# Decode attention with a Mish layer on one core: keys and values moved as whole 8 MiB units on one queue

## The chip, the cores and the metric

The kernel runs on one NeuronCore of one Trainium2 chip. The metric is the device time of one execution in microseconds (us), lower is better. Device memory feeds the core's on-chip memory (128 partitions) through 16 DMA engines. TensorE (PE) multiplies, VectorE (DVE) and ScalarE (ACT) work on the results, GpSimd (POOL) only clears buffers here, SyncE (SP) issues transfers. TensorE's products land in PSUM, in banks of 128 partitions by 512 f32.

## The reference

One decode step for 8 sequences, all f32. `x` is 8 rows of 512; 32 query heads share 8 key/value heads (4 per group); the caches hold 8192 positions of 128 numbers for each sequence and key/value head, 256 MiB of keys and 256 MiB of values.

```python
xn = layernorm(x)                                   # eps 1e-5
q  = (xn @ wq) as 8 x 32 heads x 128
p  = softmax(q . k * 128**-0.5)                     # over 8192 positions
o  = p . v
h  = xn @ w1 + b1                                   # 512 -> 1792
out = x + o @ wo + mish(h) @ w2                     # mish(h) = h * tanh(softplus(h))
```

The host lays the arrays out beforehand: keys in 1024 blocks of 128 dims x 1024 positions, values in 1024 blocks of 128 x 1024 numbers, 8 blocks for each sequence and head.

## The kernel before

The work is a list of items (L479 to L502), each a transfer into one of nine 16 KiB-per-partition buffers named `kv` (L54, L81) and the work on it. Key units `(n, b, s)` are half the positions of one head and one sequence, 2 MiB; value units are the same halves in another order. The first 16 items of keys (all sequences and halves of head 0) run alone; from then on key units of head n+1 and value units of head n alternate, and at the end 16 value units run alone. The query weights `wq` come in four pieces, two heads each, spread over the run; `wo` comes in eight pieces, one per head; `w1` after the fourth key unit; `w2` in three pieces last. The loop at L505 issues each item's transfer six items ahead (`AHEAD`), alternating between SP's and ACT's queue (`transfer`, L84), then emits the item's work.

In a key unit a row, the piece that one partition holds contiguously, is 8 KiB (L98 to L105), in a value unit 16 KiB (L107 to L114). `project` (L196) forms the queries of one head for all sequences. `scores` (L235) multiplies a key unit with weights of 64 columns; two products share the array. All 8 sequences of a head accumulate side by side in the two-bank tiles `S[0]`, `S[1]`. After the last of them `maximum` (L258) and `weights` (L272) run once per head: the maximum over rows by two tiny transposes on PE, `exp` on ACT, and a 32x32 block transpose on DVE (L284) that brings the exponents `pt` to the partitions on which the values lie. `sums` (L294) adds up the denominators, `values` (L301) multiplies exponents with value units, four products side by side, into `O`, and picks the wanted blocks with four DVE operations (L317, L319). `merge` (L330) and `outputs` (L343) apply `wo` per head; `mish` (L368) and `down` (L419) are the dense layer, `mish` right after `w1` has come, `down` at the end. Engines wait for each other by semaphores that the Tile framework puts in; each engine works through its own instructions in order.

Of the kernel before, what the change touches and what calls it, by code (L numbers as in the profile page):

```python
# [14 lines left out]
B = 8  # L15
# [7 lines left out]

G = 4
NH = 2
UK = SK // NH
GK = UK // G
TG = GK // P
# [8 lines left out]

R = B * REP
PU = NH * B

KA = 2
WK = KA * R
QB = KA * WK
QBUFS = 3
W = BW * G // DH
W4 = 4
W2R = G * FT // 2 * FP // P  # L50

BUFS = 9
AHEAD = 6
# [3 lines left out]
def kernel(  # L57
# [16 lines left out]
    kv = ctx.enter_context(tc.tile_pool(name="kv", bufs=BUFS))  # L74
# [6 lines left out]
    def buffer():  # L81
        return kv.tile([P, G * BW], F32, name="kv")

    def transfer(t, src):  # L84

        queues.reverse()
        queues[0].dma_start(t, src)

    def load_blocks(src, lo, n):

        _, rows, width = src.shape
        t = buffer()[:rows, : n * width].rearrange("p (j f) -> p j f", j=n)
        transfer(t, src[lo : lo + n].rearrange("j p f -> p j f"))
        return t

    def load_k(n, b, s):
        lo = ((b * HKV + n) * NH + s) * G
        t = buffer().rearrange("p (j f) -> p j f", j=G // KA)  # L98
        transfer(
            t,  # L100
            kT[lo : lo + G]
            .rearrange("(j a) p f -> j (a p f)", a=KA)
            .rearrange("j (p f) -> p j f", p=P),
        )
        return t  # L105

    def load_v(n, b, s):  # L107

        lo = ((b * HKV + n) * NH + s) * G
        t = buffer()  # L110
        transfer(
            t, v[lo : lo + G].rearrange("j p f -> (j p f)").rearrange("(p f) -> p f", p=P)
        )
        return t  # L114

    w2_rows = w2.rearrange("j p f -> (j p) f").rearrange("(q i) f -> q (i f)", i=W2R)

    def load_w2(lo, hi):

        t = buffer()[:, : (hi - lo) * BW]  # L120
        transfer(t, w2_rows[:, lo * BW : hi * BW])
        return t

    x_sb = const.tile([B, D], F32, name="x_sb")
    nc.scalar.dma_start(x_sb, x)
    b1_sb = const.tile([G, FG], F32, name="b1_sb")
    nc.scalar.dma_start(b1_sb, b1.rearrange("(g f) -> g f", g=G))


    items = []  # L130


    S = [psum.tile([P, GK], F32, name=f"s{i}") for i in range(NH)]
    O = [psum.tile([P, 512], F32, name=f"o{i}") for i in range(2)]
# [4 lines left out]
    ones = const.tile([P, P], F32, name="ones")  # L139

    gsel = const.tile([G, G, B], F32, name="gsel")

    rsel = const.tile([P, R], F32, name="rsel")

    hsel = const.tile([P, REP], F32, name="hsel")

    isel = const.tile([P, W4], F32, name="isel")
    qT = [const.tile([P, B * (QB + 1)], F32, name=f"qT{i}") for i in range(QBUFS)]
    xnT = const.tile([P, CC, B], F32, name="xnT")
    acc = const.tile([P, P], F32, name="acc")  # L150
    aT = const.tile([P, 2 * W2R, Q], F32, name="aT")

    def setup():
        make_identity(nc, ident)
        nc.gpsimd.memset(ones, 1.0)
        for t in qT:
            nc.gpsimd.memset(t, 0.0)
        nc.vector.memset(M, 0.0)
        nc.vector.memset(H, 0.0)
        for o in O:  # L160
            nc.vector.memset(o, 0.0)

        st = const.tile([B, 8], F32, name="st")
        xc = const.tile([B, D], F32, name="xc")
        sq = const.tile([B, D], F32, name="sq")
        nc.vector.reduce_sum(st[:, 0:1], x_sb, axis=AX.X)
        nc.vector.tensor_scalar_mul(st[:, 1:2], st[:, 0:1], 1.0 / D)
        nc.vector.tensor_scalar(xc, x_sb, st[:, 1:2], None, op0=ALU.subtract)
        nc.scalar.activation(sq, xc, AF.Square, accum_out=st[:, 2:3])
        nc.vector.tensor_scalar(  # L170
            st[:, 3:4], st[:, 2:3], 1.0 / D, EPS, op0=ALU.mult, op1=ALU.add
        )
        nc.scalar.activation(st[:, 4:5], st[:, 3:4], AF.Sqrt)
        nc.vector.reciprocal(st[:, 5:6], st[:, 4:5])

        nc.vector.tensor_mul(st[:, 6:7], st[:, 5:6], st[:, 5:6])
        nc.vector.tensor_mul(st[:, 7:8], st[:, 6:7], st[:, 3:4])
        nc.vector.tensor_scalar(st[:, 6:7], st[:, 7:8], -0.5, 1.5, op0=ALU.mult, op1=ALU.add)
        nc.vector.tensor_mul(st[:, 4:5], st[:, 6:7], st[:, 5:6])
        nc.vector.tensor_scalar(xc, xc, st[:, 4:5], None, op0=ALU.mult)  # L180
        for c in range(CC):
            nc.tensor.transpose(  # L182
                M[:, c * B : (c + 1) * B], xc[:, c * P : (c + 1) * P], ident[:B, :B]
            )
        nc.vector.tensor_copy(xnT.rearrange("p c b -> p (c b)"), M[:, : CC * B])

        nc.vector.tensor_copy(
            gsel, ident[:G, :G].rearrange("p (g o) -> p g o", o=1).to_broadcast([G, G, B])
        )
        nc.vector.reduce_sum(rsel, ident.rearrange("p (g r) -> p r g", g=G), axis=AX.X)  # L190
        used = rsel[:, : W4 * REP]
        nc.vector.reduce_sum(hsel, used.rearrange("p (i h) -> p h i", h=REP), axis=AX.X)
        nc.vector.reduce_sum(isel, used.rearrange("p (i h) -> p i h", h=REP), axis=AX.X)


    def project(n, w):  # L196

        for c in range(CC):
            for h in range(REP):
                lo = (n % 2 * REP + h) * DH  # L200
                nc.tensor.matmul(  # L201
                    H[Q * h : Q * h + B, 384:512],
                    xnT[:, c, :],
                    w[:, c, lo : lo + DH],
                    start=(c == 0),
                    stop=(c == CC - 1),
                )

        qs = work.tile([P, KA, KA, DH // KA], F32, name="qs")
        for a in range(KA):  # L210
            nc.vector.tensor_scalar_mul(  # L211
                qs[:, :, a, :],
                H[:, 384:512].rearrange("p (i r) -> p r i", r=KA),
                DH**-0.5,
            )
        for k in range(KA):
            nc.tensor.transpose(  # L217
                H[:, k * P : (k + 1) * P], qs[:, k].rearrange("p a i -> p (a i)"), ident
            )

        t = qT[n % QBUFS].rearrange("p (b c) -> p c b", c=QB + 1)
        half = P // KA
        for a in range(KA):
            for k in range(KA):
                lo = k * WK + a * R
                nc.vector.tensor_copy(  # L226
                    t[half * a : half * (a + 1), lo : lo + R : B, :],
                    H[half * a : half * (a + 1), k * P : (k + 1) * P].rearrange(
                        "p (h q) -> p h q", h=REP
                    )[:, :, :B],  # L230
                )

    NM = {}

    def scores(n, b, s, k):  # L235

        for c in range(GK // 512):
            for i in range(KA):
                w = QB * b + WK * i
                for j in range(G // KA):  # L240
                    at = i * BW + c * 512
                    nc.tensor.matmul(  # L242
                        S[s][WK * j : WK * (j + 1), c * 512 : (c + 1) * 512],
                        qT[n % QBUFS][:, w : w + WK],
                        k[:, j, at : at + 512],
                        start=(b == 0 and i == 0),
                        stop=(b == B - 1 and i == KA - 1),
                    )
        if b == B - 1:
            if s == 0:  # L250
                NM[n] = work.tile([P, NH], F32, name="nm")
            nc.vector.tensor_reduce(  # L252
                NM[n][:, s : s + 1], S[s], axis=AX.X, op=ALU.max, negate=True
            )

    NX, PT, RT = {}, {}, {}

    def maximum(n):  # L258

        nmb = work.tile([P, 1], F32, name="nmb")  # L260
        nc.vector.tensor_reduce(nmb, NM[n], axis=AX.X, op=ALU.min)
        nc.tensor.transpose(M[:1, 0:P], nmb, ident)
        nr = work.tile([1, Q], F32, name="nr")
        nc.vector.tensor_reduce(
            nr, M[:1, 0:P].rearrange("p (g q) -> p q g", g=G), axis=AX.X, op=ALU.min
        )
        nx = NX[n] = work.tile([1, G, Q], F32, name="nx")
        nc.vector.tensor_copy(
            nx, nr.rearrange("p (o q) -> p o q", o=1).to_broadcast([1, G, Q])
        )  # L270
# [286 lines left out]
```

## Time and profile before

| what | value |
|---|---|
| time, median of 3 runs | 1342.06 us (1341.81 to 1342.19) |
| profiled execution, span from first to last instruction | 1340.1 us |
| moved by DMA | 561.81 MB, mean 419 GB/s over the span |
| busy: PE, PE weight loads, DVE, ACT, POOL | 920.3, 267.1, 179.1, 23.8, 3.5 us |
| mean granted TensorE clock | 0.843 |

The profile is of one execution, whose span is 2 us shorter than the median time. Its page cuts the span in 40 equal slices (33.5 us each); a digit is the busy share in tenths, GB/s is what the DMA engines moved. A line of a group names source line, engine, operation, output <- inputs, shapes and count, then total busy time, mean ns of one, and idle time before it with what ended it. A line of the timeline begins with start and length in us and merges equal instructions (`x16`). A line of windows gives, for a stretch of time, the busy time of each engine, the granted TensorE clock, the DMA share and GB/s. A line of DMA issues ends with KB each and the median us from issue to landing. f32 products show as two instructions each.

### The profile page before, as it was taken

The page shows a single profiled execution, that of the slowest core. Times are in us where ns is not written, and L with a number is a line of the kernel's source. Part 1 is how long each engine was busy: PE and PEld are TensorE (multiplying, and loading weights), DVE is VectorE, ACT ScalarE, POOL GpSimd, SP SyncE. Part 2 cuts the span into 40 slices and gives each one's busy share as a digit, 9 for nine tenths or more (in the row PEclk, how much of TensorE's full clock was granted, in tenths as well). Part 3 has the DMA queues.
Part 4 walks back from the last instruction along what each step waited for, and adds up shares of the span by engine and source line. Part 5 has one row for each costly group of instructions (what it writes and reads, how often), then busy time and mean ns, then how long its engine had stood idle before and what let it go on. Part 6 is the DMA issues. An engine that isn't in the chain of part 4 may idle for free.

```text
span 1340.1 us, 11019 instructions
## 1 busy us (share of the span) xinstructions
PE 920.3 (69%) x4948; PEld 267.1 (20%) x4948; DVE 179.1 (13%) x443; ACT 23.8 (2%) x39; POOL 3.5 (0%) x10
## 2 busy tenths in 40 slices
PE   3778759574766856766667776676757687567766
PEld 1222212121112212212112221221212122112212
DVE  2212011020100201111010120102100020010311
ACT  1000000000000000000000000000000000000000
POOL 1000000000000000000000000000000000000000
PEclk9888879797788967988787897887878888788878
DMA  9999999999999999999999999999999999999996
GB/s 385 419 422 424 426 421 424 422 425 425 426 424 420 427 423 423 424 423 425 425 426 427 419 425 422 423 426 422 424 425 424 424 424 427 424 423 424 428 427 269
DMA packets 59240, 561.81 MB, mean 419 GB/s; under 512 B 4396, under 2 KB 4528, under 8 KB 9784
## 3 DMA queue, kind: packets, MB, share of 16 engines
q10 hardware_dynamic: 29608, 281.31, 50.0%
q1 hardware_dynamic: 29584, 279.78, 49.8%
q8 instruction: 39, 0.64, 0.2%
q14 instruction: 9, 0.07, 0.0%
HBM read 561.01 MB, written 0.07 MB: 419 GB/s over the span
## 4 chain that ended last, share of the span: by engine, by line
DMA 78%; PE 17%; another core or an unknown queue 4%; DVE 1%; issue 0%; ACTq 0%; ACT 0%; SPq 0%
DMA kv<-in_kT 62%; DMA kv<-in_v 12%; PE s L242 10%; PE o L308 5%; DMA kv<-in_w 2%; DMA kv<-in_wq 1%; PE h L201 1%; PE h L423 0%; PE m L356 0%; PE m L332 0%; PE h L217 0%; DVE pt L284 0%; PE m L295 0%; DVE os L317 0%
## 5 line engine op out<-in xcount | busy, mean ns | idle before, releaser
L242 PE MATMUL s<-kv,qT 128*64 128x512 f32 x2048 | 603.2, 730 | 307.3 <-DMA kv<-in_kT 303.7
L242 PEld LDWEIGHTS s<-kv,qT 128*64 128x64 f32 x2048 | 166.4, 166 | 711.4 <-DMA kv<-in_kT 369.6
L308 PE MATMUL o<-kv,pt 128*16 128x512 f32 x2048 | 265.5, 624 | 41.4 <-DMA kv<-in_v 39.1
L317 DVE TENSOR_SCALAR os<-o,isel 128x128 f32<-128x128 f32 x64 | 22.5, 351 | 703.2 <-PE o L308 703.2
L308 PEld LDWEIGHTS o<-kv,pt 128*16 128x16 f32 x2048 | 56.2, 114 | 190.3 <-issue 139.9
L319 DVE SCALAR_TENSOR_TENSOR os<-o,isel,os 128x128 f32<-128x128 f32 x192 | 67.1, 350 | 6.2
L252 DVE TENSOR_REDUCE nm<-s 128x1 f32<-128x1024 f32 x16 | 19.6, 1225 | 298.7 <-PE s L242 298.7
L283 ACT ACTIVATE e<-s,nmx 128x1024 f32<-128x1024 f32 x16 | 17.7, 1110 | 1187.6 <-DVE nmx L277 864.5
L201 PE MATMUL h<-kv,xnT 128*8 128x128 f32 x256 | 12.7, 362 | 37.2 <-DMA kv<-in_wq 37.2
L284 DVE STREAM_TRANSPOSE pt<-e 128x1024 f32<-128x1024 f32 x16 | 31.6, 2018 | 1.4 <-ACT e L283 1.3
L332 PEld LDWEIGHTS m<-hsel,os 128*128 128x128 f32 x128 | 19.3, 190 | 59.8 <-issue 44.9
L332 PE MATMUL m<-hsel,os 128*128 128x4 f32 x128 | 24.9, 265 | 8.5 <-DVE os L319 8.5
L201 PEld LDWEIGHTS h<-kv,xnT 128*8 128x8 f32 x256 | 7.7, 112 | 46.3 <-DMA kv<-in_wq 28.7
L211 DVE TENSOR_SCALAR qs<-h 128x128 f32<-128x128 f32 x16 | 4.2, 286 | 49.9 <-PE h L201 49.9
L356 PE MATMUL m<-kv,oT 128*8 128x128 f32 x256 | 8.9, 275 | 0.3 <-DVE oT L337 0.3
L378 PE MATMUL h<-kv,xnT 128*8 128x448 f32 x32 | 4.9, 742 | 6.0 <-DMA kv<-in_w 6.0
L356 PEld LDWEIGHTS m<-kv,oT 128*8 128x8 f32 x256 | 6.2, 89 | 5.3 <-DVE r L297 4.4
L226 DVE COPY qT<-h 64x32 f32<-64x32 f32 x32 | 5.0, 208 | 15.1 <-PE h L217 15.0
L423 PE MATMUL h<-kv,aT 128*8 128x128 f32 x112 | 5.9, 406 | 1.0 <-DMA kv<-in_w 1.0
L297 DVE RECIPROCAL r<-m 128x32 f32<-128x32 f32 x8 | 2.9, 358 | 27.1 <-PE m L295 27.1
L182 PE MATMUL m<-ident,xc 8*128 8x8 f32 x4 | 0.6, 247 | 8.2 <-DVE xc L180 8.2
L423 PEld LDWEIGHTS h<-kv,aT 128*8 128x8 f32 x112 | 4.1, 132 | 2.9 <-DMA kv<-in_w 1.4
(72 smaller groups left out, 62.1 us busy)
## 6 DMA issues: line engine op xcount, KB each, us to landing
kv<-in_kT SPq DMA_DIRECT2D x64, 2048.0 KB, 34.1
kv<-in_kT ACTq DMA_DIRECT2D x64, 2048.0 KB, 38.5
kv<-in_v ACTq DMA_DIRECT2D x64, 2048.0 KB, 27.9
kv<-in_v SPq DMA_DIRECT2D x64, 2048.0 KB, 27.9
kv<-in_wq ACTq DMA_DIRECT2D x2, 2048.0 KB, 18.2
kv<-in_wq SPq DMA_DIRECT2D x2, 2048.0 KB, 51.1
kv<-in_wo ACTq DMA_DIRECT2D x4, 1024.0 KB, 40.5
kv<-in_wo SPq DMA_DIRECT2D x4, 1024.0 KB, 35.9
```

The lines of the kernel that those rows point to most:

```text
L201: nc.tensor.matmul(H[Q * h : Q * h + B, 384:512], xnT[:, c, :], w[:, c, lo : lo + DH], start=(c == 0), stop=(c == CC - 1),)
L226: nc.vector.tensor_copy(t[half * a : half * (a + 1), lo : lo + R : B, :], H[half * a : half * (a + 1), k * P : (k + 1) * P].rearrange("p ( ...
L242: nc.tensor.matmul(S[s][WK * j : WK * (j + 1), c * 512 : (c + 1) * 512], qT[n % QBUFS][:, w : w + WK], k[:, j, at : at + 512], start=(b == ...
L252: nc.vector.tensor_reduce(NM[n][:, s : s + 1], S[s], axis=AX.X, op=ALU.max, negate=True)
L283: nc.scalar.activation(e[:, s], S[s], AF.Exp, bias=nmx, accum_out=l[:, s : s + 1])
L284: nc.vector.transpose(pt[:, s].rearrange("p (m t r) -> p t m r", m=m, t=TG), e[:, s].rearrange("p (t q m) -> p t m q", t=TG, m=m),)
L308: nc.tensor.matmul(o[Q * c : Q * c + W4 * REP, :], PT[n][:, s, W4 * R * j + b : W4 * R * (j + 1) : B], vt[:, 512 * j : 512 * (j + 1)], sta ...
L317: nc.vector.tensor_scalar(os, o[:, :DH], isel[:, 0:1], None, op0=ALU.mult)
L319: nc.vector.scalar_tensor_tensor(os, o[:, DH * i : DH * (i + 1)], isel[:, i : i + 1], os, op0=ALU.mult, op1=ALU.add,)
L332: nc.tensor.matmul(M[:, 168 + b * REP : 168 + (b + 1) * REP], OS.pop((n, b)), hsel, start=True, stop=True)
L356: nc.tensor.matmul(M[Q * g : Q * g + B, 256:384], oT[n][:, h, :], w[:, h // 2, h % 2 * D + g * P : h % 2 * D + (g + 1) * P], start=(h == 0 ...
L423: nc.tensor.matmul(H[Q * g : Q * g + B, :P], aT[:, j, :B], w[:, at : at + P], start=(j == 0), stop=(j == 2 * W2R - 1),)
```

## The change

The whole schedule is rewritten; the host's layout and the result are the same. A **unit** is now one sequence `b` and a pair of heads `m`: 16 blocks, 8 MiB of keys or of values, moved by one transfer in which each partition gets 64 KiB (`ROW`) contiguously. There are 32 units. All transfers but the two smallest (`x`, `b1`) are issued by SP. On-chip there is one array `kv` of 160 KiB per partition: keys of even units at 0, of odd ones at 32 KiB, so that neighbouring units share half their place, and one place for values behind them. Three of the four `wq` pieces come first, into the place of the values, then the first keys, then `w1` and the last `wq` piece.

```diff
-BUFS = 9
-AHEAD = 6
+NB = 2 * NH * G                  (16 blocks a unit)
+ROW = NB * P * BW // P           (16384 f32)
+DI = ROW // BW                   (16)
+K_AT = (0, ROW // 2)
+V_AT = ROW + ROW // 2
+PLACES = V_AT + ROW
...
-    queues = [nc.sync, nc.scalar]
+    ctx.enter_context(tc.manual_schedule())
+    kv = const.tile([P, PLACES], F32, name="kv")
+    S = psum.tile([P, 512], F32, name="s")
+    X = psum.tile([P, 4, 512], F32, name="x4")
+    O = psum.tile([P, 512], F32, name="o")
...
+    def load_pair(src, m, at):
+        t = kv[:, at : at + 4096]
+        rows = src.rearrange("j p f -> (j p f)").rearrange("(m p f) -> m p f", m=NP, p=P)
+        nc.sync.dma_start(t, rows[m])
+    def load_unit(src, j, at):
+        m, b = divmod(j, B)
+        lo = (b * HKV + 2 * m) * NH * G
+        t = kv[:, at : at + ROW]
+        nc.sync.dma_start(t, src[lo : lo + NB].rearrange("j p f -> (j p f)")
+                             .rearrange("(p f) -> p f", p=P))
...
+    def project(m):
+        for d in range(2):
+            for c in range(CC):
+                nc.tensor.matmul(H[Q * c : Q * c + B, :], xn4[:, c, :],
+                                 w[:, c, d * 512 : (d + 1) * 512], start=True, stop=True)
+            nc.scalar.copy(qp, H)
+            for h in range(REP):
+                nc.tensor.matmul(M[:, at : at + B], qp[:, h * DH : (h + 1) * DH], bsel[:, :B], ...)
+        nc.vector.tensor_scalar_mul(qT, M[:, 192 : 192 + H2 * B], DH**-0.5)
+        for half in range(2):
+            for k in range(8):
+                nc.tensor.matmul(X[:, half, k * 64 : (k + 1) * 64], wide[:, half * 8 + k :: DI], qT, ...)
+            nc.scalar.copy(qr[:, m, half * 8 : (half + 1) * 8]..., X[:, half])
+    def key_weights(j):
+        for d in range(2):
+            nc.vector.tensor_mul(w[:, :, d], q[:, :, d]..., mask[...]...)      (512 elements each)
+    def scores(j, k, first, part):
+        lo = 0 if first else DI // 2
+        for n in range(DI // 2):
+            for c in range(HALF):
+                nc.tensor.matmul(S[64 * c : 64 * (c + 1), :], w[:, lo + n]..., kk[:, lo + n, c, :],
+                                 start=(part == 0 and n == 0), stop=(part == 1 and n == DI // 2 - 1))
+    def softmax(j):        (maximum of S, two transposes on PE, exp of 128 x 512 on ACT, lsel)
+    def turn(j, lsel):
+        for g in range(4):
+            nc.tensor.matmul(X[:, g], perm[:, g], e, start=True, stop=True)
+        nc.tensor.matmul(M[:, 136 : 136 + H2], ones, lsel, start=True, stop=True)
+        nc.vector.reciprocal(RT[j], M[:, 136 : 136 + H2])
+        for tl in range(TL):
+            nc.vector.transpose(tr...[:, tl], X...[:, tl])                   (512 elements each)
+        for d in range(2):
+            nc.vector.tensor_reduce(pt8[half...], tr[half]..., axis=AX.X, op=ALU.add)  (2048 in)
+    def values(j, vt):     (32 products of 32 columns into O, then the four DVE operations)
+    def merge(j, os):
+        nc.tensor.matmul(M[:, 168 : 168 + H2], os, hsel, start=True, stop=True)
+        nc.vector.tensor_mul(oT[:, m, :, b], M[:, 168 : 168 + H2], RT.pop(j))
...
+    for m in range(NP - 1):
+        project(m)
+        if m == 0:
+            key_weights(0)
+    (w1, b1 and the last piece of wq are loaded)
+    for j in range(UNITS):
+        scores(j, k, j % 2 == 1, 0)
+        if j + 1 < UNITS:
+            k_t[j + 1] = load_k(j + 1)
+        else:
+            v_t[j] = load_unit(v, j, 0)
+        scores(j, k, j % 2 == 0, 1)
+        lsel = softmax(j)
+        if j > 0:
+            os = values(j - 1, v_t.pop(j - 1))
+        else:
+            mish(w1_t, b1_sb, kv[:, V_AT + 8192 : V_AT + 12288 - FG])
+            project(NP - 1)
+        if j + 1 < UNITS:
+            v_t[j] = load_unit(v, j, V_AT)
+            key_weights(j + 1)
+        turn(j, lsel)
+        if j > 0:
+            merge(j - 1, os)
+    (wo in four pieces into the place of the values, w2 in three into that of the keys)
+    (values of the last unit, all output products into X[:, 0], down per piece of w2)
```

The text in round brackets stands for code that is left out or for sizes. The scores of a unit fill one bank, `S`: its 128 rows are two halves of 512 positions, two heads, eight blocks and four query heads. Exponents and values of a unit lie on different partitions; `turn` brings them together with four products against the permutation matrices `perm`, four block transposes and two reductions, where before one block transpose per half did it. The setup also builds `perm` (eight small copies), `mask`, `bsel`, `isel`, `rsel` and `hsel` (six reductions), `wide` and a second set of transposed inputs, `xn4`. `mish` is unchanged but keeps its intermediate tiles in the place of the values. The products with `wo` all run after the last unit, and their result is added to `H` by four products with `bsel`.

More of the change, by code (lines that the diff above doesn't have):

```diff
@@ L196, in project @@
[L196 to L270, printed above, removed]
@@ new lines @@
+    for c in range(CC):
+        nc.tensor.transpose(
+            M[:, 32 + c * B : 32 + (c + 1) * B], xc[:, c * P : (c + 1) * P], ident[:B, :B]
+        )
+    nc.vector.tensor_copy(xn4.rearrange("p c b -> p (c b)"), M[:, 0:32])
+    nc.vector.tensor_copy(xnT.rearrange("p c b -> p (c b)"), M[:, 32:64])
+    for g in range(G):
+        nc.tensor.matmul(
+            M[Q * g : Q * g + B, 256:384],
+            ident[:B, :B],
+            x_sb[:, g * P : (g + 1) * P],
+            start=True,
+            stop=True,
+        )
@@ L368, in mish @@
-    def mish(ws):
+                tr.rearrange("p (l t) c -> p t l c", t=TL)[:, tl],
+                X.rearrange("p g (t q l) -> p t l g q", t=TL, q=PP)[:, tl],
+            )
+        for d in range(2):
+            half = slice(64 * d, 64 * (d + 1))
+            nc.vector.tensor_reduce(
+                pt8[half, :, :, d * REP : (d + 1) * REP].rearrange("p c y h -> p y c h"),
+                tr[half].rearrange("p y (g c h) -> p y c h g", g=4, c=HALF),
+                axis=AX.X,
+                op=ALU.add,
+            )
@@ new lines, in values @@
+    def values(j, vt):
+        for n in range(NJ):
+            l, c = divmod(n, HALF)
+            q = n % G
+            nc.tensor.matmul(
+                O[Q * q : Q * (q + 1), :],
+                pt8[:, c, TL * l : TL * (l + 1), :].rearrange("p t h -> p (t h)"),
+                vt[:, 512 * n : 512 * (n + 1)],
+                start=(n < G),
+                stop=(n >= NJ - G),
+            )
+        os = work.tile([P, DH], F32, name="os")
+        nc.vector.tensor_scalar(os, O[:, :DH], isel[:, 0:1], None, op0=ALU.mult)
+        for i in range(1, TL):
+            nc.vector.scalar_tensor_tensor(
+                os, O[:, DH * i : DH * (i + 1)], isel[:, i : i + 1], os, op0=ALU.mult, op1=ALU.add
+            )
+        return os
@@ new lines @@
+    os = values(UNITS - 1, v_t.pop(UNITS - 1))
+    for m in range(NP - 1):
+        outputs(m, w_o[m])
+    merge(UNITS - 1, os)
+    outputs(NP - 1, w_o[NP - 1])
+    a_sb = work.tile([P, 512], F32, name="e")
+    nc.scalar.copy(a_sb, A)
+    down(*parts[0], w2_t[0])
+    for g in range(G):
+        nc.tensor.matmul(
+            H[Q * g : Q * g + B, :P],
+            bsel[:, :B],
+            a_sb[:, g * P : (g + 1) * P],
+            start=False,
+            stop=False,
+        )
+    for p, t in zip(parts[1:], w2_t[1:]):
+        down(*p, t)
@@ L516 @@
     res = const.tile([P, P], F32, name="res")
[L517 removed]
+    nc.vector.tensor_add(res, H[:, :P], xres)
     nc.sync.dma_start(out, res)
```

441 lines of the change are left out of this document (196 added, 245 removed).

## The prediction, made before the changed kernel was run

> **What bounds the kernel now.** First the page: its slices, its queues and the chain that ended last.
>
> ```profile
> PEclk9888879797788967988787897887878888788878
> DMA  9999999999999999999999999999999999999996
> GB/s 385 419 422 424 426 421 424 422 425 425 426 424 420 427 423 423 424 423 425 425 426 427 419 425 422 423 426 422 424 425 424 424 424 427 424 423 424 428 427 269
> ...
> q10 hardware_dynamic: 29608, 281.31, 50.0%
> q1 hardware_dynamic: 29584, 279.78, 49.8%
> ...
> DMA 78%; PE 17%; another core or an unknown queue 4%; DVE 1%; issue 0%; ACTq 0%; ACT 0%; SPq 0%
> ```
>
> The 16 DMA engines are busy in every slice but the last, at about 424 GB/s, and the two queues' packets fill 99.8% of their time. The chain is transfers of keys and values. So the time is the bytes over the rate, plus the ends, and the bytes do not change. What the change can move is the rate, and whether the engines always have a transfer queued.
>
> Next, does the rate depend on the row length? Before, a key transfer has rows of 8 KiB and a value transfer rows of 16 KiB. The first value transfer is issued at 81.68 us, and the last key tile was waited for at 1250.82, so there is a stretch with keys alone and one with values alone.
>
> ```profile
> kv<-in_kT SPq DMA_DIRECT2D x64, 2048.0 KB, 34.1
> kv<-in_kT ACTq DMA_DIRECT2D x64, 2048.0 KB, 38.5
> kv<-in_v ACTq DMA_DIRECT2D x64, 2048.0 KB, 27.9
> kv<-in_v SPq DMA_DIRECT2D x64, 2048.0 KB, 27.9
> ...
> 81.68 20.33 ACTq L87 DMA_DIRECT2D kv<-in_v  x3
> ...
> 1250.82 5.35 PE L242 MATMUL s<-kv,qT 128*64 128x512 f32 x16 [4.67 <-DMA kv<-in_kT]
> ...
> 60.00:80.00 20.00, 14.17 (x64) 4.42 (x64) 7.04 (x8) 0.00 (x0) 0.00 (x0) 1.00 1.02 421
> 100.00:400.00 300.00, 210.49 (x1094) 60.64 (x1090) 36.80 (x90) 4.60 (x8) 0.00 (x0) 0.84 1.01 424
> 1250.00:1310.00 60.00, 41.82 (x256) 11.09 (x256) 14.97 (x36) 2.30 (x4) 0.00 (x0) 0.77 1.01 427
> ```
>
> Rows of 8 KiB run at 421, rows of 16 KiB at 427, and the mixture at 424 (the last number of each window). One engine, a sixteenth of that, spends 8192 x 16 / 421 = 311.3 ns on an 8 KiB row and 613.9 ns on a 16 KiB row. The second 8 KiB cost 302.6 ns, so 8.7 ns of each row do not depend on its length.
>
> **Term 1, the rate.** A 64 KiB row would take 8 x 302.6 + 8.7 = 2429.5 ns, which is 431.6 GB/s. The 256 transfers of 2048 KB are 536.9 MB: 1266.2 us at 424, 1243.9 at 431.6, a gain of **22.3 us**. Bounds: with no cost per row at all 433.2 GB/s (gain 26.8); with no gain beyond 16 KiB rows 427 (gain 8.8); no gain at 424; and a loss of 9 at 421, if long rows were read like the keys. I take 431.6, since both steps that the trace has go that way. Query weights also go from 4 KiB to 16 KiB rows, 1536 rows fewer: 1536 / 16 x 8.7 ns = **0.8 us** gained.
>
> **Term 2, is a transfer always queued?** Before, six tiles are on their way. Now one unit is 8 MiB of keys and 8 MiB of values, each 19.4 us at 431.6, and three things follow each other on SP's in-order queue: next keys (which wait for the first half of this unit's score products, whose place they take), then values (which wait for all value products of the unit before, as there is one place for values), and so on. PE's own order is scores A, scores B, two tiny transposes for the maximum, value products of the unit before, four permutation products, merge.
>
> ```profile
> 29.80 13.09 PE L242 MATMUL s<-kv,qT 128*64 128x512 f32 x58
> 634.53 6.51 PE L242 MATMUL s<-kv,qT 128*64 128x512 f32 x16 [8.33 <-DMA kv<-in_kT]
> 1273.55 3.64 PE L308 MATMUL o<-kv,pt 128*16 128x512 f32 x32
> 1293.14 6.55 PE L308 MATMUL o<-kv,pt 128*16 128x512 f32 x32 [3.15 <-DMA kv<-in_v]
> ...
> L252 DVE TENSOR_REDUCE nm<-s 128x1 f32<-128x1024 f32 x16 | 19.6, 1225 | 298.7 <-PE s L242 298.7
> L284 DVE STREAM_TRANSPOSE pt<-e 128x1024 f32<-128x1024 f32 x16 | 31.6, 2018 | 1.4 <-ACT e L283 1.3
> L283 ACT ACTIVATE e<-s,nmx 128x1024 f32<-128x1024 f32 x16 | 17.7, 1110 | 1187.6 <-DVE nmx L277 864.5
> L332 PE MATMUL m<-hsel,os 128*128 128x4 f32 x128 | 24.9, 265 | 8.5 <-DVE os L319 8.5
> ```
>
> Each f32 product shows as two instructions (1024 score products in the code, x2048 in the page). PE at full clock takes 13.09 / 58 = 0.226 us per score instruction and 3.64 / 32 = 0.114 per value instruction; after idling it starts at half that pace (6.51 / 16 = 0.41, 6.55 / 32 = 0.20). The counts stay: 64 and 64 instructions per unit, so 14.4 and 7.3 us warm. Four permutation products over the whole array are 8 passes of 0.43 us (two 64-column passes shared 2 x 0.226 = 0.45): 3.6 us, all added. With the keys landed at 0: scores A until about 9 (cold at first), so the next keys are issued at 9 and, with 1.6 us to start, are ready 9 us before the queue runs dry at 19.4; scores B until 16.2; the maximum and its transposes (half of L252's 1.23 us, then three steps of under 0.5 us) until 19; values land at 21; their products until 28.3, 9 us before the next keys have landed at 38.8. Permutations until 32. DVE gets, per unit, four transposes of 512 (half of 2018 ns each, 4.0), two reductions of 2048 elements (2 x 2.45), the two weight masks (2 x 0.7), the merge steps and the maximum: about 14 us of 38.8, and what is last, the exponents in the values' order, is ready near 42, when it is needed at 60. So inside the loop everything new is covered by transfers, with some 9 us to spare on either issue; were the cover gone, the permutations and DVE's turn would cost 12.5 us a unit. **0 us.**
>
> **Term 3, the start.** Nothing covers PE and SP there.
>
> ```profile
> 0.74 0.92 SPq L87 DMA_DIRECT2D kv<-in_kT  x2
> 8.79 0.19 DVE L185 COPY xnT<-m 128x32 f32<-128x32 f32 x1 [0.75 <-PE m L182]
> 29.43 0.20 PEld L217 LDWEIGHTS h<-ident,qs 128*128 128x128 f32 x2 [1.55 <-issue]
> 42.82 0.93 PE L373 MATMUL h<-b_sb,gsel 4*8 4x448 f32 x8
> 43.69 1.69 PE L378 MATMUL h<-kv,xnT 128*8 128x448 f32 x16
> 51.43 3.17 PE L378 MATMUL h<-kv,xnT 128*8 128x448 f32 x16 [6.05 <-DMA kv<-in_w]
> 54.67 0.62 DVE L386 COPY mh<-h 128x448 f32<-128x448 f32 x1 [24.04 <-PE h L378]
> 60.80 2.95 DVE L407 RECIPROCAL mz<-ma 128x448 f32<-128x448 f32 x1
> ...
> L190 DVE TENSOR_REDUCE rsel<-ident 128x32 f32<-128x128 f32 x1 | 0.3, 350 | 0.0
> 0.00:10.00 10.00, 0.56 (x4) 0.50 (x4) 5.36 (x19) 3.49 (x5) 3.54 (x10) 1.00 0.83 305
> ```
>
> Data flow from 2.8 us (305 GB/s over the first ten at 423). Query weights, keys 0, w1 and the last query weights, 6.3 + 8.4 + 3.7 + 2.1 MB, end at 2.8 + 14.7 + 19.4 + 8.8 + 4.9 = 50.6. The next transfer, keys 1, waits for scores A of unit 0, and PE first has three whole projections to do (before: one, and the keys came in 2 MiB pieces). DVE's setup ends at 8.98 plus six reductions of 0.35, eight copies like L185 (0.19) and four more transposes: 13. One projection is, for each of two heads, 8 instructions of 512 columns (half of 1.69 or 3.17 by 512/448: 0.97 to 1.81), a copy on ACT of 0.6 with 0.2 of hand-over, 8 weight loads of 128 columns (0.10 each by L217's pair, to 0.195 by half of L332's two instructions, 0.39 in the chain of a merge); then 32 more such loads. That is 8.7 to 15 us; I take 13, because these short products leave the array mostly loading and the clock low. So scores A start at 13 + 39 = 52, end at 60, and data come at 61.6: a gap of 11 us (0 to 22). Second gap: values 0 wait for the mish work, which now lies in their place. After scores A: scores B 7.2, maximum 2.4, mish products 4.4 to 7.3 (L373 and two of L378), DVE's chain from 54.67 to 63.75 and three more steps, 11.4; with the start 27 to 30, while keys 1 end at 21: 7.5 (6 to 9). Behind it, PE waits with the last projection's second half for DVE, and the permutations and scores A of unit 1 stand behind that: keys 2 come 0 to 8 late, I take 2. By unit 2 the queue is ahead. **Cost 20 us** (6 to 39).
>
> **Term 4, the end.**
>
> ```profile
> 1331.22 5.85 PE L423 MATMUL h<-kv,aT 128*8 128x128 f32 x112 [1.03 <-DMA kv<-in_w]
> 1337.47 0.35 SPq L518 DMA_DIRECT2D out<-res  x1
> out<-res SPq DMA_DIRECT2D x1, 64.0 KB, 1.6
> ```
>
> On two queues the three w2 parts land together, and all 112 instructions follow. In one queue's order the last part leaves 16 of them (0.8 us) and some backlog; I count 2.4 in place of 5.9, a gain of **3.5** (0 to 5).
>
> **The sum.** 1340.1 - 22.3 - 0.8 + 0 + 20 - 3.5 = 1333.5 for an execution like the profiled one, whose span lies 2.0 below the median of the runs: **1335.5 us**. Its own range is 1328 to 1343.
>
> **Rivals.** (a) *Long rows are not read faster.* Sixteen engines then read rows whose starts lie at larger powers of two apart and may meet in the same part of memory. At 424 the sum is 1357.8, at 427 it is 1349.0; the gaps and the end decide the sign at 429.3 GB/s, so this is the rival that ends slower. Against it: the pitch doubled from keys to values and the rate rose. The Trainium skill, "DMA: Bandwidth & Descriptors", section "Latency and other measured facts", warns of large power-of-two row pitches and gives 207 against 214 GB/s at 512 KiB, growing with the pitch; if that 3.3% held here, an estimate is 417 GB/s and some 1378 us. No run so far has a 64 KiB pitch. (b) *One queue leaves a hole at each of 64 transfers.* At most the 1.6 us of the lone last transfer each: 102 us, some 1438; but the next transfer is queued 9 us ahead, so an engine need not wait for a landing. The same page, "Issuing engines are not separate DMA queues", says that several issuing engines save only issue time; by it this rival is nothing, and the trace before never shows one queue alone. (c) *PE becomes the bound*: at half clock throughout, 64 x 0.41 + 64 x 0.20 + 7.2 + 3 = 49 us against 38.8, some 10 us for each unit so run, 1500 if half of them are; the slices' clock of 0.7 to 0.9 with gaps of up to 8 us speaks against it, bursts now being longer. (d) *The projections run at full clock*: gaps of 8, 1323.5. (e) *The projections are slower than my bound* (weights read in steps of 16): gaps of 35, 1350.
>
> **Chances.** Forecast 0.50, (a) 0.22, (b) 0.05, (c) 0.03, (d) 0.15, (e) 0.05. The range takes (d) with the upper rate, 1340.1 - 26.8 - 0.8 + 8 - 4.5 + 2 = 1318, and (a) at 424, 1358. This measurement tells about 0.2%, 2.7 us, from no change: faster is below 1339.4. That has four fifths of the forecast and all of (d), 0.55; within, 0.11 (the forecast's upper edge and (a) at its best); slower 0.34.
>
> **What would show it.** Right: slices of 430 to 433 GB/s from the fourth on; two or three slices of the first four well below that; waits of SP on PE for scores A that end well ahead of the landing; DVE under 45% busy. Wrong: a rate of 427 or less in the middle (a); a DMA share under 1.0 between units with the next issue already done (b), or with SP still waiting for PE (c).

## The result, and the profile after

The changed kernel takes 1344.25 us (median of 13 runs, 1342.08 to 1347.79) beside 1341.04 us for the kernel before on the same chips: a ratio of 1.0026, 95% interval 1.0018 to 1.0034. It is slower by 3.2 us (0.26%, small but clear of the interval), where 6.6 us faster was forecast. The profiled execution spans 1342.5 us.

The page of the changed kernel: clock, DMA share and GB/s in 40 slices of 33.6 us, and the one queue that is left (packets, MB, share of the time of 16 engines).

```profile
PEclk9988888889988888888888789878888978887898
DMA  9569999999999999999999999999999999999997
GB/s 407 204 282 405 436 432 418 436 438 429 432 436 435 434 426 434 432 434 438 436 426 430 434 426 434 436 436 436 432 432 436 421 438 438 426 434 430 434 417 319
...
q1 hardware_dynamic: 13520, 561.06, 97.1%
```

From the fifth slice on the rate is about 433 GB/s, more than forecast. The second and third slices hold a hole. How much each is worth shows when both kernels are cut in the same three stages, start, loop and end (busy time of PE, PEld, DVE, ACT and POOL, granted clock, DMA share, GB/s). First before:

```profile
0.00:140.00 140.00, 95.58 (x474) 29.40 (x476) 27.28 (x61) 7.65 (x11) 3.54 (x10) 0.93 1.00 414
140.00:1290.00 1150.00, 793.47 (x4180) 226.65 (x4176) 144.02 (x359) 16.10 (x28) 0.00 (x0) 0.84 1.01 424
1290.00:1343.00 53.00, 31.23 (x298) 11.09 (x298) 7.80 (x23) 0.00 (x0) 0.00 (x0) 0.79 0.73 305
```

and after, with the ten-microsecond windows of the start in which the DMA share is low:

```profile
0.00:140.00 140.00, 110.67 (x530) 61.16 (x530) 40.20 (x85) 16.24 (x27) 2.20 (x9) 0.93 0.78 327
140.00:1290.00 1150.00, 855.42 (x4184) 278.21 (x4184) 454.43 (x622) 22.89 (x59) 0.00 (x0) 0.87 1.00 433
1290.00:1343.00 53.00, 33.61 (x326) 11.25 (x326) 13.80 (x19) 1.06 (x3) 0.00 (x0) 0.87 0.84 348
...
30.00:40.00 10.00, 8.13 (x37) 5.62 (x34) 1.63 (x3) 1.17 (x2) 0.00 (x0) 1.00 0.83 335
50.00:60.00 10.00, 8.25 (x37) 6.17 (x36) 0.22 (x1) 1.17 (x2) 0.00 (x0) 1.00 0.07 29
60.00:70.00 10.00, 10.00 (x38) 5.48 (x40) 0.00 (x0) 0.59 (x1) 0.00 (x0) 1.00 0.01 2
70.00:80.00 10.00, 9.34 (x44) 2.81 (x40) 0.61 (x1) 0.00 (x0) 0.00 (x0) 1.00 0.80 315
90.00:100.00 10.00, 4.47 (x22) 4.38 (x23) 8.61 (x11) 0.59 (x1) 0.00 (x0) 0.56 0.56 211
110.00:120.00 10.00, 10.00 (x42) 3.69 (x42) 7.29 (x7) 0.00 (x0) 0.00 (x0) 0.92 0.73 315
```

In the first 140 us the changed kernel moves 87 x 0.140 = 12.2 MB less, 28.7 us at the old rate. The rates of the loop are printed in whole GB/s, which is coarse for a stage that long; the mean of its 115 windows of ten microseconds is 424.1 before and 432.7 after. So in the loop the changed kernel moves 8.6 x 1.150 = 9.8 MB more, 23.2 us. At 1290 it is thus some 5.5 us behind, and it ends 2.4 behind, so the end gained some 3. The shares that are missing in the six windows add up to 1.7 + 9.3 + 9.9 + 2.0 + 4.4 + 2.7 = 30 us.

What PE does in the hole is in the timeline of the changed kernel (start, length, instructions). The first projection and the first score products, SP's issues of keys 1, values 0 and keys 2, and the first steps of the last projection:

```profile
11.45 1.90 PE L209 MATMUL h<-kv,xn 128*8 128x512 f32 x8
14.05 1.88 PE L220 MATMUL m<-bsel,e 128*128 128x8 f32 x8 [0.70 <-ACT e L217]
20.65 3.73 PE L232 MATMUL x<-qT,tr 128*128 128x64 f32 x16 [0.32 <-DVE qT L228]
28.72 1.90 PE L209 MATMUL h<-kv,xn 128*8 128x512 f32 x8
63.51 15.83 PE L267 MATMUL s<-kv,wk 128*64 128x512 f32 x64
66.98 0.24 PEld L267 LDWEIGHTS s<-kv,wk 128*64 128x64 f32 x2 [0.62 <-issue]
68.02 0.14 PEld L267 LDWEIGHTS s<-kv,wk 128*64 128x64 f32 x2 [0.29 <-issue]
72.56 0.33 SPq L118 DMA_DIRECT2D kv<-in_kT  x1
86.11 1.04 PE L209 MATMUL h<-kv,xn 128*8 128x512 f32 x8 [0.75 <-DVE kv L366]
87.92 1.06 PE L220 MATMUL m<-bsel,e 128*128 128x8 f32 x8 [0.76 <-ACT e L217]
96.88 0.33 SPq L118 DMA_DIRECT2D kv<-in_v  x1
119.62 0.33 SPq L118 DMA_DIRECT2D kv<-in_kT  x1
```

One projection takes 28.72 - 11.45 = 17.3 us. Three of them hold scores A back to 63.5 us, and keys 1 are issued at 72.6, when the queue has been empty for some 20 us. The same eight instructions that take 1.90 and 1.88 us here take 1.04 and 1.06 us after the mish products: the first three projections ran at half clock throughout. The score products behind them show the step up: their pairs of weight loads (PEld) come every 0.86 us at 66.98 (0.24 of load and 0.62 of idle time) and every 0.43 us at 68.02.

### The profile page after: what moved, and what is told of

Read it like the earlier page. It is cut to its first block, busy times and chain, and to the rows that moved or that the text cites. A ratio compares the mean times of both kernels' runs of the same rounds, so it can differ in the third digit from the quotient of the medians.

```text
span 1342.5 us, 11144 instructions
## 1 busy us (share of the span) xinstructions
PE 999.7 (74%) x5040; PEld 350.6 (26%) x5040; DVE 508.4 (38%) x724; ACT 40.2 (3%) x88; POOL 2.2 (0%) x9
## 4 chain that ended last, share of the span: by engine, by line
DMA 70%; PE 26%; DVE 2%; SPq 2%; ACT 1%; issue 0%; ACTq 0%
DMA kv<-in_v 68%; PE o L329 19%; PE x L232 2%; PE s L267 2%; DMA kv<-in_w 2%; SPq L467 1%; PE m L220 1%; PE h L209 1%; PE x L306 0%; ACT e L217 0%; PE h L358 0%; ACT qr L239 0%; DVE kv L380 0%; DVE nm L279 0%; ACT L172 0%
## 5 line engine op out<-in xcount | busy, mean ns | idle before, releaser
L267 PE MATMUL s<-kv,wk 128*64 128x512 f32 x2048 | 512.0, 664 | 199.9 <-DMA kv<-in_kT 199.9
L329 PE MATMUL o<-kv,pt 128*32 128x512 f32 x2048 | 262.1, 670 | 49.7 <-DMA kv<-in_v 40.1
L267 PEld LDWEIGHTS s<-kv,wk 128*64 128x64 f32 x2048 | 157.2, 153 | 529.4 <-issue 326.6
L317 DVE TENSOR_REDUCE pt<-tr 64x512 f32<-64x2048 f32 x64 | 241.3, 3771 | 1.6
L329 PEld LDWEIGHTS o<-kv,pt 128*32 128x32 f32 x2048 | 68.9, 121 | 216.5 <-issue 164.1
L306 PE MATMUL x<-e,perm 128*128 128x512 f32 x256 | 121.3, 617 | 0.8 <-ACT qr L239 0.8
L337 DVE TENSOR_SCALAR os<-o,isel 128x128 f32<-128x128 f32 x32 | 11.2, 351 | 262.7 <-PE o L329 262.7
L311 DVE STREAM_TRANSPOSE tr<-x 128x512 f32<-128x512 f32 x128 | 78.6, 670 | 0.0
L306 PEld LDWEIGHTS x<-e,perm 128*128 128x128 f32 x256 | 47.1, 194 | 74.5 <-issue 74.5
L250 DVE TENSOR_TENSOR wk<-qr,mask 128x512 f32<-128x512 f32 x64 | 62.9, 1025 | 8.9 <-ACT qr L239 8.9
L232 PE MATMUL x<-qT,tr 128*128 128x64 f32 x128 | 29.9, 426 | 8.5 <-DVE qT L228 5.8
L339 DVE SCALAR_TENSOR_TENSOR os<-o,isel,os 128x128 f32<-128x128 f32 x96 | 33.7, 351 | 3.4
L232 PEld LDWEIGHTS x<-qT,tr 128*128 128x128 f32 x128 | 28.4, 309 | 9.6 <-DVE qT L228 6.1
L220 PE MATMUL m<-bsel,e 128*128 128x8 f32 x64 | 13.8, 344 | 6.0 <-ACT e L217 6.0
L220 PEld LDWEIGHTS m<-bsel,e 128*128 128x128 f32 x64 | 13.0, 301 | 18.5 <-ACT e L217 18.5
```

The costliest lines, as they stand in the source:

```text
L220: nc.tensor.matmul(M[:, at : at + B], qp[:, h * DH : (h + 1) * DH], bsel[:, :B], start=True, stop=True,)
L232: nc.tensor.matmul(X[:, half, k * 64 : (k + 1) * 64], wide[:, half * 8 + k :: DI], qT, start=True, stop=True,)
L250: nc.vector.tensor_mul(w[:, :, d], q[:, :, d].to_broadcast([P, DI, NH * G, REP]), mask[:, d * NH * G : (d + 1) * NH * G] .rearrange("p (o ...
L267: nc.tensor.matmul(S[64 * c : 64 * (c + 1), :], w[:, i].rearrange("p d k h -> p (d k h)"), kk[:, i, c, :], start=(part == 0 and n == 0), s ...
L306: nc.tensor.matmul(X[:, g], perm[:, g], e, start=True, stop=True)
L311: nc.vector.transpose(tr.rearrange("p (l t) c -> p t l c", t=TL)[:, tl], X.rearrange("p g (t q l) -> p t l g q", t=TL, q=PP)[:, tl],)
```

## The experiments

Times are medians; "before" is the kernel before on the same chip. Unless said otherwise each kernel is the changed one with one edit.

**Is the start the loss?** `one_projection` leaves out the projections of heads 2 to 5 (their queries are zero).

```diff
-    for m in range(NP - 1):
-        project(m)
-        if m == 0:
-            key_weights(0)
+    project(0)
+    key_weights(0)
```

> The changed kernel with projections 1 and 2 left out (the queries of heads 2 to 5 are zero); all transfers stay. My theory: the three projections ahead of unit 0, 17.3 us each, are the whole start gap; with one, scores A of unit 0 begin near 31 in place of 63.5 us, keys 1 are issued near 40, before the last query weights have landed, and the later two holes close with it. Then the first 140 us move at over 420 GB/s in place of 327 and the time falls by 24 to 31 us, to 1313 to 1320. Rival: the hole is the start of the single queue or of the long rows itself, and the time stays within 10 us of 1344.

1322.21 us, ratio 0.9851 (0.9835 to 0.9867): 22 us gone, 2 short of what was expected. In its windows the large hole is closed. Contrary to my expectation the two later ones did not close with it; they only come earlier, 4.4 us at values 0 behind the mish work and 2.1 us at keys 2 behind the last projection:

```profile
70.00:80.00 10.00, 5.98 (x26) 5.70 (x26) 6.92 (x8) 0.59 (x1) 0.00 (x0) 0.50 0.56 212
90.00:100.00 10.00, 10.00 (x50) 3.35 (x48) 9.66 (x6) 0.00 (x0) 0.00 (x0) 1.00 0.79 315
```

`late_projections` leaves nothing out. The projections of heads 2 to 7 move into the loop, and the mish work to where its result holds nobody back. `project` is cut in two, `spread` being its second half (the products with `wide`, rebuilt by `widen`).

```diff
+    (w1 is loaded right behind keys 0)
+    spread(0, project(0))
+    key_weights(0)
     for j in range(UNITS):
         scores(j, k, j % 2 == 1, 0)
+        if j in (3, 5, 7):
+            qT = project(j // 2)
+            widen()
         (keys j + 1 are loaded)
+        if j == 0:
+            mish(w1_t, b1_sb, ...)
         scores(j, k, j % 2 == 0, 1)
+        if j in (2, 4, 6):
+            wq_t[j // 2] = load_pair(wq, j // 2, 0)
...
+        if qT is not None:
+            spread(j // 2, qT)
         turn(j, lsel)
```

> The result is the same. Only the query weights of heads 0 and 1 come ahead of unit 0; the other three pieces are loaded in units 2, 4 and 6 into the half of the keys' place that is free between an even and the next even unit, and projected in units 3, 5 and 7, where PE waits for keys anyway; w1 is loaded right behind keys 0 and the mish work is done between scores A and scores B of unit 0. My theory: the start gap was the whole loss, so with scores A of unit 0 at about 31 us the holes shrink to some 4 us in all and the time is 1314 to 1322, below both kernels. Rival: projections in the loop make the next keys or values late by 3 to 8 us each and mish holds unit 0 back, so that 10 us or more come back: 1326 or more.

1319.14 us, ratio 0.9835 (0.9821 to 0.9849), below both kernels. The start moves at 404 GB/s, the loop at 432; what is left of the holes is mainly the one ahead of keys 1:

```profile
0.00:140.00 140.00, 98.26 (x480) 39.08 (x480) 60.96 (x107) 10.03 (x17) 2.21 (x9) 0.93 0.95 404
140.00:1290.00 1150.00, 879.96 (x4326) 305.13 (x4330) 448.99 (x615) 29.61 (x70) 0.00 (x0) 0.87 1.00 432
...
30.00:40.00 10.00, 8.56 (x30) 2.68 (x32) 1.39 (x2) 0.73 (x1) 0.00 (x0) 1.00 0.62 245
```

So where PE would otherwise wait for keys, the projections cost nothing that shows. Where SP waits for PE, two of them had cost some 22 us, by the run before. The rest of the 25 us goes with the mish work and the last projection, which no longer hold up values 0 and keys 2.

`late_projections_2` also fills that hole: the second piece of query weights goes behind `w1`, into the place of the first, and is projected in unit 0.

```diff
+    qT = project(0)
+    wq_t[1] = load_pair(wq, 1, V_AT + 4096 * (NP - 1))
+    spread(0, qT)
...
+        if j == 0:
+            qT = project(1)
         lsel = softmax(j)
```

> As late_projections, but the second piece of query weights is loaded behind w1, into the place of the first, and projected in unit 0 while DVE does the mish work, so that 4.9 us of transfer fill the hole ahead of keys 1 (3.8 us at 30 to 40 us). My theory: the hole closes and the time falls by another 3 to 5 us, to 1314 to 1316. Rival: values 0 then wait for the second projection and the hole moves there: 1318 to 1322.

1317.26 us, ratio 0.9824 (0.9809 to 0.9838): 1.9 us better, not 3 to 5 (it ran on another chip than `late_projections`; the kernel before has the same median, 1340.62 us, on both). The hole at 30 is closed, but half of it comes back at 80, where keys 2 are issued late because the second projection now stands on PE ahead of scores A of unit 1:

```profile
30.00:40.00 10.00, 8.56 (x32) 2.65 (x32) 1.39 (x2) 0.73 (x1) 0.00 (x0) 1.00 1.04 423
80.00:90.00 10.00, 8.93 (x43) 2.70 (x39) 5.99 (x5) 0.00 (x0) 0.00 (x0) 1.00 0.81 321
```

**Is it the row that sets the rate?** `rows_16k` issues a unit as four transfers, `rows_8k` as eight.

```diff
+        part = ROW // 4                        (8 in rows_8k)
+        for i in range(4):
+            nc.sync.dma_start(t[:, i * part : (i + 1) * part], rows[:, i * part : (i + 1) * part])
```

> Each unit's transfer is issued as four, of 16 KiB rows each, on the same queue into the same place; nothing else changes. My theory: the row's length sets the rate, so the loop falls from 433 to about 427 GB/s, and 536.9 MB take 17 us more: 1358 to 1364. Rival: the single queue, or one stream at a time in place of two, gave the rate; then it stays at 433 and the time within 3 us of 1344.

> Each unit's transfer is issued as eight, of 8 KiB rows each, on the one queue. My theory: a fixed cost of 8.7 ns for each row gives about 421 to 423 GB/s in the loop (64 KiB 433, 16 KiB 428). Rival: with one queue the length does not matter below 16 KiB, or the size of a transfer matters and not that of a row: the loop is at 428, or below 418.

`rows_16k` takes 1349.47 us, ratio 1.0062 (1.0047 to 1.0077); `rows_8k`, in a single run, 1366.97 us. The loop and some windows of the start of `rows_16k`:

```profile
0.00:140.00 140.00, 110.48 (x529) 60.66 (x529) 39.79 (x84) 16.24 (x27) 2.21 (x9) 0.93 0.84 351
140.00:1290.00 1150.00, 845.86 (x4218) 262.78 (x4218) 455.28 (x623) 23.35 (x60) 0.00 (x0) 0.90 1.01 428
...
90.00:100.00 10.00, 4.16 (x25) 3.83 (x21) 8.88 (x12) 0.59 (x1) 0.00 (x0) 0.59 1.02 433
110.00:120.00 10.00, 10.00 (x40) 3.61 (x41) 6.85 (x7) 0.00 (x0) 0.00 (x0) 0.89 1.02 436
```

and the loop of `rows_8k`:

```profile
140.00:1290.00 1150.00, 873.37 (x4168) 253.13 (x4166) 451.82 (x614) 22.57 (x58) 0.00 (x0) 0.89 1.01 421
```

421, 428 and 433 GB/s for rows of 8, 16 and 64 KiB on one queue: the two-term law of the prediction holds. Worked out again from the finer means of the loops, 421.2 and 432.7, a row costs some 9.5 ns and 301.7 ns for every 8 KiB, which gives 427.7 at 16 KiB, as measured. It is the row and not the size of the transfer: 8 KiB rows run at 421 in transfers of 1 MiB on one queue here and in transfers of 2 MiB on two queues in the kernel before, and 2 MiB transfers of 16 KiB rows ran there at 427. The time of `rows_16k` was missed: 14.5 us of the loop are lost as expected (536.9 MB at 428 and 433), but 9 are won back. Its start moves 24 x 0.140 = 3.4 MB more, 8 us, and the holes at 90 and 110 are gone: pieces of values 0 and keys 2 are issued as soon as their part of the place is free.

**Does the queue matter?** `two_queues` puts values on ACT's queue; `two_queues_16k` does the same on top of `rows_16k`.

```diff
-        nc.sync.dma_start(
+        (nc.scalar if src is v else nc.sync).dma_start(
```

> Values go to ACT's queue, keys stay on SP's; rows of 64 KiB and all waits as they are. My theory: the number of queues does nothing for the rate, the loop stays at 431 to 434 GB/s and the time within 4 us of 1344. Rival: a single queue is what helps (two streams disturb each other) or what hurts (a hole between transfers): then the rate moves by 4 GB/s or more and the time by 10 us or more.

> Values on ACT's queue and keys on SP's, every unit in four transfers with rows of 16 KiB. If two streams of 64 KiB rows disturb each other within an engine, shorter rows end that: the loop at 424 to 428 GB/s, as in the kernel before or on one queue, and no idle engines. If the loss with two queues is that keys and values no longer come in turn, so that landings come too late for the single places, it stays: the loop at 422 or less.

`two_queues`: 1361.14 us, ratio 1.0145 (1.0118 to 1.0171); `two_queues_16k`, in a single run: 1358.27 us. The loop of the first:

```profile
140.00:1290.00 1150.00, 800.86 (x4130) 268.40 (x4128) 451.12 (x621) 22.58 (x58) 0.00 (x0) 0.85 0.99 426
```

and of the second:

```profile
140.00:1290.00 1150.00, 848.39 (x4190) 270.18 (x4192) 456.58 (x622) 22.59 (x58) 0.00 (x0) 0.88 1.01 428
```

My theory fell here: with rows of 64 KiB a second queue costs 6.5 GB/s (426.2 beside 432.7 by windows of ten microseconds), 17 us over the loop, and the DMA share drops below 1.00. With rows of 16 KiB two queues give the 428 GB/s that one gives, so in the loop two queues are no loss in themselves (this kernel is 9 us behind `rows_16k`, 8 of them by its start, which moves 327 GB/s in place of 351). Whether it is the long rows that disturb each other or whole units that, sharing the engines, land too late for their single places stays open: the 16 KiB version changes the row and the size of a transfer together, and my expectation overlooked that. The traces also hold the time of every row, and they show some of both. In the loop of `two_queues` 4.3% of the 64 KiB rows take more than 2.6 us, beside 0.6% in the changed kernel; all rows together take each engine some 9.5 us longer. And 15.91 rows are under way on average in place of 16.03, which is some 8.5 us of idle engines.

**Is the loop's new work really covered?** `double_turn` does the permutation products twice.

```diff
-        for g in range(4):
+        for g in (0, 1, 2, 3, 0, 1, 2, 3):
             nc.tensor.matmul(X[:, g], perm[:, g], e, start=True, stop=True)
```

> The four permutation products of each unit are done twice, with the same result. My theory: transfers cover them with some 6 us of PE idle before the next keys, so 32 times 3.7 us more PE work cost nothing in the loop and 4 to 7 us at unit 0, where nothing covers them: 1344 to 1351. Rival: PE's order is close to the path; then each unit grows by some of the 3.7 us and the time by 30 us or more.

1348.24 us, ratio 1.0058 (1.0041 to 1.0075), 4 us more than the changed kernel, as expected: 2.6 us of it in the start, which moves 319 GB/s in place of 327. The loop stands:

```profile
140.00:1290.00 1150.00, 965.26 (x4429) 325.00 (x4428) 455.50 (x620) 22.58 (x58) 0.00 (x0) 0.90 1.00 432
```

PE is busy 110 us longer in that stage, at 432 GB/s.

**Why were the projections slow?** `wide_filler` puts a 512-column product after every second narrow one of the spreading step. `plain_weights` stores the selection matrices so that the 128 weight columns lie side by side. `plain_filler` does both.

```diff
-                    wide[:, half * 8 + k :: DI],
+                    wide[:, (half * 8 + k) * P : (half * 8 + k + 1) * P],      (plain)
...
+                if k % 2 == 1:                                                   (filler)
+                    nc.tensor.matmul(X[:, 2 + half], ident, wide[:, 0:512], start=True, stop=True)
```

> The changed kernel with one more product of 512 columns (into an unused bank) after every second narrow product of the spreading step of each projection, 8 per projection. My theory: the weight loads of the projections took 0.30 us each because narrow products leave TensorE's clock at half; wide products between them raise it, and the loads of that line fall from 309 ns to about 190 to 200, as the loads of the permutation products have, though each projection does more. Rival: the loads are slow because their columns are taken in steps of 16; then they stay near 309 ns.

> The changed kernel with the selection matrices of the spreading step stored so that each product's 128 weight columns lie side by side in place of 16 apart; same result. If the step of 16 made the weight loads slow, they fall from 309 ns to 190 to 200, each spreading step from 7.5 to 4 to 5 us, and three of them ahead of unit 0 plus one inside the second hole take 10 to 14 us off: 1330 to 1334. If the half clock did, nothing changes while no wide product stands between: 1342 to 1346.

> Both: columns side by side and the eight 512-column products in each projection. If both the step and the clock hold the loads, only here they fall below 250 ns; if the step alone does, they are as in plain_weights; if neither, 300 ns and more remain.

`plain_weights`: 1343.76 us, ratio 1.0021 (1.0011 to 1.0031), no change; the fillers cost more than they bring, 1367.52 and 1359.08 us in a single run each. The groups of weight loads (busy us, mean ns of one) in the changed kernel (those of its permutation products, L306, take 194 ns):

```profile
L232 PEld LDWEIGHTS x<-qT,tr 128*128 128x128 f32 x128 | 28.4, 309 | 9.6 <-DVE qT L228 6.1
L220 PEld LDWEIGHTS m<-bsel,e 128*128 128x128 f32 x64 | 13.0, 301 | 18.5 <-ACT e L217 18.5
```

with the fillers (`wide_filler`):

```profile
L232 PEld LDWEIGHTS x<-qT,tr 128*128 128x128 f32 x128 | 32.6, 308 | 26.2 <-issue 11.7 <-DVE qT L228 6.3 <-ACT qr L241 6.0
L220 PEld LDWEIGHTS m<-bsel,e 128*128 128x128 f32 x64 | 9.5, 228 | 15.1 <-ACT e L217 15.1
```

with plain columns (`plain_weights`):

```profile
L232 PEld LDWEIGHTS x<-qT,tr 128*128 128x128 f32 x128 | 27.9, 330 | 8.1 <-DVE qT L228 4.6 <-ACT qr L239 3.5
```

and with both (`plain_filler`):

```profile
L232 PEld LDWEIGHTS x<-qT,tr 128*128 128x128 f32 x128 | 22.4, 226 | 25.3 <-issue 14.8 <-ACT qr L241 6.0 <-DVE qT L228 4.5
```

These means mix both clocks, because the fillers raise the clock only for part of each projection. The timelines keep them apart: the pair of filler instructions (L240) takes 2.02 us at half clock and 1.08 at the raised one. Four narrow ones (L232) beside them, at half clock and then at the raised one, in `wide_filler`:

```profile
23.40 0.95 PE L232 MATMUL x<-qT,tr 128*128 128x64 f32 x4
24.14 2.02 PE L240 MATMUL x<-tr,ident 128*128 128x512 f32 x2
32.11 0.87 PE L232 MATMUL x<-qT,tr 128*128 128x64 f32 x4
32.81 1.08 PE L240 MATMUL x<-tr,ident 128*128 128x512 f32 x2
```

and in `plain_filler`, at the raised clock:

```profile
30.28 0.55 PE L232 MATMUL x<-qT,tr 128*128 128x64 f32 x4
30.68 1.08 PE L240 MATMUL x<-tr,ident 128*128 128x512 f32 x2
```

My theory that the clock alone does it was half right. L220's loads, whose columns always lay side by side, fall with the fillers from 301 to 228 ns. L232's fall only with both edits. At half clock a step of 16 costs nothing more, which is why `plain_weights` changes nothing; at the raised clock it holds four instructions at 0.87 us where plain columns take 0.55. So the half clock set the pace in this kernel, and the step of 16 would have set it next. An estimate from these rows: at the raised clock with the step a projection would take 2 x (1.04 + 1.06) + 32 x 0.217 + 2.3 = 13.4 us, without it 2 x (1.04 + 1.06) + 32 x 0.138 + 2.3 = 10.9, in place of 17.3.

## Why the prediction was wrong

**Term 1, the rate, was right, and 3 us small.** 432.7 GB/s in place of 431.6, and 424.1 before in place of 424, make 25.1 us in place of 22.3. The long pitch did no harm (rival a, given 0.22). The Trainium skill's warning, "DMA: Bandwidth & Descriptors", section "Latency and other measured facts", begins at pitches of 512 KiB; here, at 64 KiB, the trace shows no loss. Rival (b) is out too: the DMA share in the loop is 1.00 on one queue.

**Term 2, nothing to pay in the loop, was right.** One unit in the middle of the changed kernel, with the costliest of the added groups:

```profile
618.20 0.33 SPq L118 DMA_DIRECT2D kv<-in_kT  x1
628.10 7.07 PE L329 MATMUL o<-kv,pt 128*32 128x512 f32 x64 [1.04 <-DMA kv<-in_v]
635.23 0.33 SPq L118 DMA_DIRECT2D kv<-in_v  x1
...
L317 DVE TENSOR_REDUCE pt<-tr 64x512 f32<-64x2048 f32 x64 | 241.3, 3771 | 1.6
```

Keys are issued 10 us before the values ahead of them have landed, so the queue does not run dry; the forecast had 9 to spare. The reductions took 3.8 us each and not 2.45, which nobody waits for: DVE is at 38%. The doubled permutations confirm the cover by experiment.

**Term 3, the start, is the step that failed.** It was put at 20 us, with 13 us for a projection, "8.7 to 15"; a projection took 17.3 us, above that bound, and the holes came to 30 us. The prediction named the low clock as its reason for 13, and yet priced the weight loads, in both bounds, by rows at full clock. The upper one took 0.195 us a load from the merge (L332) of the kernel before, which runs inside the loop:

```profile
L332 PEld LDWEIGHTS m<-hsel,os 128*128 128x128 f32 x128 | 19.3, 190 | 59.8 <-issue 44.9
```

Loads of this shape last 190 ns there and 330 ns at half clock (L232 in `plain_weights`). Overlapped as they are, eight instructions of L220 in 1.88 us and sixteen of L232 in 3.73 come to 0.234 us each: 48 of them make 11.2 us, L209 twice 3.8, the copies and hand-overs 2.3 (1.6 forecast), together 17.3. By the estimate above 13 is about the time of a projection at the raised clock. Scores A thus began at 63.5 and not at 52, and keys 1 were issued at 72.6 and not at 60. The first hole grew from 11 us to 21. The second, 4.4 us in its window, was shorter than the 7.5 I had taken, and the third, 2.7, near the 2. A fourth, 1.7 us ahead of `w1`, I had put at nothing: `w1` goes into the place of the first two pieces of query weights, and SP waits until the second projection has read them (35.1 us).

Rival (e), with a gap of 35 and 1350, was the nearest, but not for the reason it gave: at the clock that the projections got, the step of 16 cost nothing.

**Term 4, the end, was right** as far as the windows tell: some 3 us of gain where 3.5 were forecast.

The sum with the measured terms is 1340.1 - 25.1 - 0.8 + 30 - 3 = 1341, against 1342.5 (the 0.8 of the query weights is the forecast's own, and no run tells it apart). The better rate hid 3 us of the miss. All the signs that the prediction named for being right came: the rate in the middle, two or three slow slices at the start, SP waiting for PE well ahead of the landings, DVE at 38%. None of them gave the size of the hole, which decided the sign.

The experiments show the cause from both sides: with two projections left out 22 us go, and with all of them kept, but three of them and the mish work moved, 25 us go, at a loop of 432 GB/s. That the half clock made the projections long is read from the pace of their instructions; no run here raised the clock without adding work.

## What to carry to other kernels

Longer rows raised the rate by 2% all along, and the new order of work was paid for once, at the start, where the second unit's transfer waited for three projections; count both, and put into the start only what the first consumer needs. Here, work ahead of the first wait of the busy queue was paid in full, and the same work where an engine waits for data was free. When a bound is taken from a row, ask at which clock that row ran.

## What the runs showed of the hardware

- A row cost one DMA engine a fixed time and a time per byte: 421, 428 and 433 GB/s at 8, 16 and 64 KiB, on one queue as on two up to 16 KiB. With whole units of 64 KiB rows two queues fall to 426.
- For 50 us PE was busy some 80 to 90% of each window (8.13 and 8.25 of ten in those shown) with mostly narrow products, and the clock stayed at half. The Trainium skill, "TensorE: Matmul & The Clock Gate", section "Part 1: The HAM clock gate", lets the clock rise after some 3.4 us of sustained activity; the trace agrees for wide products (the loads of scores A, begun at 63.5 us, go from one pair every 0.86 us to one every 0.43 between 67 and 68 us) and not for these (L209 still takes 1.90 us after 39 us of them, at 50.6). The granted clock of these windows reads 1.00 all the same, so there the pace of the instructions has to be read and not that column.
- Weight columns 16 apart load as fast as columns side by side at half clock (309 and 330 ns) and are the slower ones when the clock is raised (0.87 and 0.55 us for four instructions).
